# Attention with two value products in every second step, exponentials ahead of a copy, and a sixth buffer of probabilities

## The chip, the cores and the metric

The kernel runs on one core of a Trainium2 chip. The metric is device time in microseconds (us) for one launch. Before the change the median of 3 runs is 656.25 us (653.67 to 657.86).

## What is computed

An attention with a mask from hashed buckets, followed by two mixtures of experts on its output. Cut to what matters:

```python
# q, k, v: (2, 8, 768, 64) float32, proj: (64, 6)
q_bucket = sum((q @ proj > 0) * 2 ** arange(6))      # k_bucket likewise
scores = where(q_bucket == k_bucket, q @ k.T / 8, -1e9)
attn = exp(scores - max(scores)); attn = attn / (sum(attn) + 1e-9)
x = (attn @ v)            # laid out as 1536 rows of 512
x = moe(x)                # 8 experts, 192 rows each, assigned greedily by logit
out = moe2(x)             # rows with a positive skip score go to their best expert
```

## The kernel before, in words

Only the attention loop and three small places behind it are touched.

**Units and steps.** The 16 heads of queries are worked as 16 units (line 106): a pair of heads (two times 64 rows of the 128 partitions) and half of the 768 queries. A unit has 6 steps (line 354), each for 128 queries of one head against all 768 keys. One step issues, in program order:

- the scores, four matmuls in the first precision half (line 191) and the second (line 193), into a tile `S` of PSUM with 2 buffers; VectorE then takes the maximum (line 195) and two small numbers `g` and `b` (lines 196 and 197);
- splits of later queries and keys on VectorE and GpSimd (lines 130, 139, 146), by the tables `splits` and `kplan`;
- one chunk of the product with the values, `av` (line 227): a chunk is 128 keys, for both heads at once, two matmuls that fill 64 columns of the array each. After the sixth chunk ScalarE copies the result to `OT` (line 231) and VectorE computes `r` (lines 233 and 234);
- the projections for the buckets of the next unit (line 162, tile `aux`) in step 3, in some units also in step 1; VectorE turns them into bits (lines 168 and 176, "thresholds" below);
- transposes of the probabilities of two earlier steps (line 213), in tiles `pT` of PSUM with 2 buffers. One tile takes four transposes. An even step fills two tiles, an odd step one. ScalarE copies each to `PT` (line 216);
- the exponential of the step's own scores on ScalarE (line 204), which writes the probabilities `P`, 5 buffers.

In an even step the exponential stands between the copies of the two tiles. In an odd step it stands behind the copy of the one tile. Transposes of a pair of steps 2n and 2n+1 are issued in steps 2n+4 (two tiles) and 2n+5 (the third). In step 0 of units 3 to 15 a product `fin` (line 270) follows.

**What sets the order.** Each engine executes its instructions in the order in which this program issues them; the tile framework adds semaphores where a tile is written and read, or where a buffer is taken again.

**Behind the loop.** `consts` of class `Moe` (line 1070) fills part of a table `ys` in memory with zeros. `columns0` (line 1376) turns the first 128 rows of the second mixture's second tile. `tile2` (line 1397) computes one tile of the second mixture: `o` (line 1441) is the result, `ix` and `ixi` (lines 1444 and 1446) are the rows to which it goes, and `send` writes it out.

Of the kernel before, what the change touches and what calls it, by code (L numbers as in the profile page):

```python
# [7 lines left out]
F32 = mybir.dt.float32  # L8
# [5 lines left out]
ALU = mybir.AluOpType  # L14
# [9 lines left out]
class Net:  # L24
# [68 lines left out]
    def attention(self, r, later):  # L93

        nc, A = self.nc, self.A
        with self.rows as ctx:
# [2 lines left out]

            self.X = ctx.enter_context(self.pool("rows", 1)).tile([128, 12, XW], F32, name="X")  # L100
            st = ctx.enter_context(self.pool("st", 4))
            pp = ctx.enter_context(self.pool("pp", 5))
            ptp = ctx.enter_context(self.pool("ptp", 2))
            sm = ctx.enter_context(self.pool("sm", 4))
            ps = ctx.enter_context(self.pool("ps", 1, PSUM))
# [247 lines left out]
            for u in range(NU):  # L353
                for i in range(6):
                    g = u * 6 + i
                    score(u, i)
                    if (u, i) in setup:
                        setup[u, i]()
                    for f, *x in splits.get((u, i), []):
                        f(*x, ceng=nc.scalar if u == 0 else nc.vector)  # L360
                    if i == 1:
                        if u + 2 < NU:
                            loadq(u + 2)
                        for _ in kplan.get(u + 1, []):
                            if nload < len(order):
                                loadk(order[nload])
                                loadv(order[nload])
                                nload += 1
                    ua, ca = (u - 1, i - 4) if i >= 4 else (u - 2, i + 2)
                    if ua >= 0:  # L370
                        av(ua, ca)

                    if i and gens and (i == 1 or u == NU - 1 or not full[0]):
                        full[0] = next(gens[0], self)
                        if full[0] is self:
                            gens.pop(0)
                            full[0] = None
                    if left:
                        next(left, None)
                        left = None  # L380
                    if (u, i) in projs:
                        left = project(projs[u, i])
                        next(left, None)

                    gp = g - 4 if g % 2 == 0 else g - 5
                    if gp >= 0:
                        tu, ti = divmod(gp, 6)
                        for cp in ((0, 1) if g % 2 == 0 else (2,)):
                            tpose(tu, ti // 2, cp)
                            if cp == 0:  # L390
                                expo(u, i)
                    if gp < 0 or g % 2:
                        expo(u, i)
                    if i == 0 and u >= 3:
                        fin(u - 3)
                        if u - 3 in (6, 7, 11):
                            q = 3 * (6, 7, 11).index(u - 3)
                            gens.append(r.count0(q, q + 3, sm, ps, ("pT", 2, "aux")))
# [16 lines left out]
            g = r.count0(9, 11, sm, ps, tags)  # L415
# [3 lines left out]
            x = [fin_values(L - 2, UD[L]["A"][:, 384:768]), fin_values(L - 1, UD[L]["B"][:, 384:768])]  # L419
# [646 lines left out]
class Moe:  # L1066
# [3 lines left out]
    def consts(self):  # L1070
        n, nc, c = self.n, self.nc, self.n.c
        kw = dict(allow_small_or_imprecise_dtypes=True)

        self.wsg = c.tile([128, 4, 32], F32, name="wsg")
        nc.gpsimd.memset(self.wsg, 0.0)
        nc.sync.dma_start(self.wsg[:, :, 0:9], n.A["wsg"])
        self.i9 = c.tile([128, 9], F32, name="i9")
        v = nc.gpsimd
        v.tensor_tensor(self.i9, n.idf[:, 0:9], n.idf[:, 32:41], op=ALU.add)
        v.tensor_tensor(self.i9, self.i9, n.idf[:, 64:73], op=ALU.add)  # L1080
        v.tensor_tensor(self.i9, self.i9, n.idf[:, 96:105], op=ALU.add)
        self.cnt = c.tile([128, 8], F32, name="cnt2")
        nc.gpsimd.memset(self.cnt, 0.0)
        self.ecap = c.tile([128, 8], F32, name="ecap")
        nc.gpsimd.iota(self.ecap, pattern=[[1536, 8]], base=0, channel_multiplier=0, **kw)
        self.trash = c.tile([128, 1], F32, name="trash")
        nc.gpsimd.iota(self.trash, pattern=[[0, 1]], base=100000, channel_multiplier=1, **kw)
        self.par1 = c.tile([128, 1], F32, name="par1")
        nc.gpsimd.iota(self.par1, pattern=[[0, 1]], base=1, channel_multiplier=1, **kw)
        self.first = c.tile([128, 8, NB], F32, name="first")  # L1090
        nc.gpsimd.iota(self.first, pattern=[[0, 8], [128, NB]], base=128, channel_multiplier=0, **kw)
        nc.gpsimd.iota(self.first[:, 0:1, :], pattern=[[0, 1], [128, NB]], base=256, channel_multiplier=0, **kw)
        self.slot0 = c.tile([128, 2], F32, name="slot0")
        nc.gpsimd.iota(self.slot0, pattern=[[128, 2]], base=0, channel_multiplier=1, **kw)
        nc.gpsimd.iota(self.slot0[64:128, 1:2], pattern=[[0, 1]], base=128, channel_multiplier=1, **kw)

        with self.tc.tile_pool(name="zr", bufs=1, side="right") as zp:
            z = zp.tile([128, 386], F32, name="zrow")
            nc.gpsimd.memset(z, 0.0)
            zt = zp.tile([128, TROWS // 128, 4], F32, name="ztab")  # L1100
            nc.gpsimd.memset(zt, 0.0)
            nc.gpsimd.iota(zt.bitcast(I32)[:, :, 0], pattern=[[0, TROWS // 128]], base=1536, channel_multiplier=0)
            nc.sync.dma_start(n.A["tb"].rearrange("(p r) c -> p r c", p=128), zt)

            ys = n.A["ys"][1344:1537, :].rearrange("r d -> (r d)").rearrange("(h p x) -> h p x", h=2, p=128)
            for h in range(2):
                nc.sync.dma_start(ys[h], z)

    def fetch(self, res, half, q=None):

# [265 lines left out]
    def columns0(self, rows):  # L1376
# [6 lines left out]
        yield  # L1383
        for d in range(4):
            nc.tensor.matmul(pt[:, d, :], self.yr[0][:, d * 128:(d + 1) * 128], self.pick[:, 0, :], start=False, stop=False, **kw)
            nc.tensor.matmul(pt[:, d, :], self.yr[1][:, d * 128:(d + 1) * 128], self.pick[0:64, 1, :], start=False, stop=True, **kw)
        self.x0 = self.parts(pt)

# [8 lines left out]
    def tile2(self, W, rows, x, tick, nxt=None, last=False):  # L1397
# [36 lines left out]
        for f in range(8):  # L1434
# [2 lines left out]
                turn(1)  # L1437
            if f == 5 and nxt is not None:
                nx = nxt()
        o = self.m2.tile([128, 512], F32, name="o9") if last else sb.tile([128, 512], F32, name="o2", tag="yr1", bufs=2)  # L1440
        v.scalar_tensor_tensor(o, py, tb[:, 2:3], xr, op0=ALU.mult, op1=ALU.add)

        ix = sb.tile([128, 2], F32, name="ix")
        v.tensor_scalar(ix[:, 0:1], tb[:, 1:2], 0.5, self.trash, op0=ALU.is_lt, op1=ALU.mult)
        ixi = (self.m2 if last else sb).tile([128, 1], I32, name="ixi9" if last else "ixi")
        v.scalar_tensor_tensor(ixi, tb[:, 1:2], -1.0, ix[:, 0:1], op0=ALU.add, op1=ALU.add)
        if last:
            return o, ixi
        self.send(o, ixi)
# [275 lines left out]
```

## Time and profile before

| what | value |
|---|---|
| runs | 656.25 us median (653.67, 656.25, 657.86) |
| profiled execution | 658.05 us, of which span 656.3 us |
[...]
| PE (matmul) busy | 607.8 us, 93% of the span |
| PEld (weight load) busy | 423.6 us, 65% |
| DVE busy | 487.2 us, 74% |
| ACT busy | 399.7 us, 61% |
| POOL busy | 158.1 us, 24% |

The span is the time from the first to the last instruction; the 1.75 us around it are the same launch. PE is TensorE, PEld its weight loads, DVE is VectorE, ACT is ScalarE, POOL is GpSimd. A row of the timeline gives the start, the time taken, the engine, the line, the instruction with output and inputs, their shapes, how many instructions are merged in the row, and in brackets the idle time before it with what ended it. The scores of the first unit start at 7.5 us and the last step's at 257.45 us; the attention is done at about 280 us, and the two mixtures follow.

### The profile page before, as it was taken

Reading aid. Unit: us, or ns where it says so; the run is one execution under the profiler, and the core shown is the slowest. Engines: PE = TensorE matmul, PEld = TensorE weight load, DVE = VectorE, ACT = ScalarE, POOL = GpSimd, SP = SyncE. Lnnn points to the kernel's source line nnn. Section 1 sums busy time; section 2 is a strip of 40 time slices with the busy share of each in tenths; the row PEclk is TensorE's granted clock in tenths of the full one; section 3 lists DMA queues with packets and bytes.
Section 4 is the critical chain, followed back from the end, with each engine's and each line's share of the span. In section 5 each row is a group of like instructions: output and inputs, shape, how many; then the busy total and the mean of one; then the engine's idle time right before and its main releaser. Section 6 shows DMA issues by size and latency. Waiting matters only on the chain.

```text
span 656.3 us, 11406 instructions
## 1 busy us (share of the span) xinstructions
PE 607.8 (93%) x3781; PEld 423.6 (65%) x3781; DVE 487.2 (74%) x1542; ACT 399.7 (61%) x909; POOL 158.1 (24%) x212
## 2 busy tenths in 40 slices
PE   6999999999999999865878899999999999999994
PEld 3656665555566656745647486686786778877883
DVE  6888888889786786574848676867643567999991
ACT  5777777776777777412434554554554556887881
POOL 2343233332111110250103031221502322311110
PEclk8899999999999999957989899999999999999998
DMA  6214323312300010053367827558665379999800
GB/s 216 64 60 124 116 76 98 97 38 73 98 25 25 1 50 2 1 201 131 129 188 273 280 39 281 171 176 265 223 218 178 109 278 344 384 379 330 299 14 23
DMA packets 53239, 99.69 MB, mean 152 GB/s; under 512 B 6421, under 2 KB 12949, under 8 KB 53168
## 3 DMA queue, kind: packets, MB, share of 16 engines
q1 hardware_dynamic: 42016, 76.21, 35.0%
q10 hardware_dynamic: 7072, 13.63, 6.0%
q0 software_dynamic: 4080, 8.99, 4.2%
q8 instruction: 34, 0.56, 0.3%
q14 instruction: 37, 0.30, 0.2%
HBM read 88.72 MB, written 12.46 MB: 154 GB/s over the span
## 4 chain that ended last, share of the span: by engine, by line
PE 30%; DVE 10%; issue 6%; DMA 4%; ACT 2%; POOL 1%; POOLq 0%; ACTq 0%; DVEq 0%
PE ph L1166 10%; PE y L1191 6%; PE y L1197 4%; DVE wlo L1353 4%; DMA out<-o,ixi 3%; DMA xg<-xd,idsb 1%; PE pr L1235 1%; PE py L1414 1%; PE py L1413 1%; PE py L1412 1%; PE ph L1412 1%; PE pxt L1145 1%; PE ph L1413 1%; PE ph L1414 1%; ACT whi L1352 1%
## 5 line engine op out<-in xcount | busy, mean ns | idle before, releaser
L1353 DVE TENSOR_TENSOR wlo<-w,whi 128x512 fp32r<-128x512 f32 x192 | 123.6, 685 | 22.6 <-ACT whi L1352 20.8
L216 ACT ACTIVATE PT<-pT 128x512 f32<-128x512 f32 x135 | 79.8, 595 | 52.8 <-PE pT L213 52.1
L195 DVE TENSOR_REDUCE nm<-S 128x1 f32<-128x768 f32 x96 | 91.8, 956 | 25.9 <-PE S L193 24.1
L1352 ACT ACTIVATE whi<-w 128x512 fp32r<-128x512 f32 x192 | 109.4, 622 | 0.4 <-issue 0.4
L1166 PE MATMUL ph<-xT,w 128*128 128x192 f32 x512 | 103.0, 345 | 4.5 <-PEq L1518 4.5
L204 ACT ACTIVATE P<-S,b,g 128x768 f32<-128x768 f32 x96 | 94.7, 987 | 13.3 <-DVE b L197 11.7
L213 PEld LDWEIGHTS pT<-idf,P 128*128 128x128 f32 x576 | 62.4, 142 | 51.4 <-issue 30.7
L1166 PEld LDWEIGHTS ph<-xT,w 128*128 128x128 f32 x512 | 84.1, 195 | 14.9 <-issue 10.2
L213 PE MATMUL pT<-idf,P 128*128 128x128 f32 x576 | 84.7, 282 | 0.7 <-ACT PT L219 0.3
L227 PE MATMUL av<-PT,vd 128*64 128x384 f32 x360 | 77.5, 511 | 0.0
L191 PE MATMUL S<-K,Q 128*128 128x512 f32 x192 | 58.7, 387 | 5.3 <-ACT P L204 4.1
L146 POOL TENSOR_TENSOR Q<-qd,Q 64x384 fp32r<-64x384 f32 x30 | 31.0, 1033 | 134.2 <-PE pT L213 73.1
L1171 ACT ACTIVATE h<-ph 128x128 f32<-128x128 f32 x64 | 17.7, 276 | 60.0 <-PE ph L1166 30.7
L193 PE MATMUL S<-K,Q 76*128 76x512 f32 x192 | 51.0, 347 | 1.8 <-DVE Q L168 1.8
L191 PEld LDWEIGHTS S<-K,Q 128*128 128x128 f32 x192 | 29.7, 194 | 10.6 <-issue 5.8
L193 PEld LDWEIGHTS S<-K,Q 76*128 76x128 f32 x192 | 30.4, 195 | 6.4 <-issue 2.1
L139 POOL TENSOR_TENSOR K<-kd,K 64x768 fp32r<-64x768 f32 x15 | 27.2, 1815 | 26.3 <-DVE K L130 14.5
L1197 PE MATMUL y<-w,h 128*64 128x512 f32 x128 | 33.2, 624 | 0.0
L227 PEld LDWEIGHTS av<-PT,vd 128*64 128x64 f32 x360 | 18.0, 134 | 22.7 <-issue 19.2
L1314 POOL DMA_INDIRECT tb<-rec,ii x16 | 15.9, 996 | 64.7 <-DVE cnt L1311 48.5
L1414 PE MATMUL py<-whi,hl 128*128 128x512 f32 x72 | 29.3, 407 | 1.4 <-DVE hl L1423 1.3
L1412 PE MATMUL py<-whi,hh 128*128 128x512 f32 x72 | 29.9, 415 | 0.0
(374 smaller groups left out, 1100.6 us busy)
## 6 DMA issues: line engine op xcount, KB each, us to landing
w<-w SPq DMA_DIRECT2D x28, 1024.0 KB, 8.5
w<-u SPq DMA_DIRECT2D x26, 1024.0 KB, 9.6
kd<-kT SPq DMA_DIRECT2D x16, 384.0 KB, 4.7
qd<-qT SPq DMA_DIRECT2D x32, 192.0 KB, 3.8
w<-u ACTq DMA_DIRECT2D x6, 1024.0 KB, 13.2
w<-w ACTq DMA_DIRECT2D x4, 1024.0 KB, 7.6
xd<-X SPq DMA_DIRECT2D x4, 780.0 KB, 4.2
vd<-v SPq DMA_DIRECT2D x16, 192.0 KB, 4.0
```

Of the source, the lines that this page charges most:

```text
L191: nc.tensor.matmul(S[:, n0:n1], d["Q1", a][:, ts], kd["K1"][:, n0:n1], start=True, stop=False)
L193: nc.tensor.matmul(S[:, n0:n1], d["Q2", a][:, ts], kd["K2"][:, n0:n1], start=False, stop=True)
L195: nc.vector.tensor_reduce(d["nm"][:, c], S, op=ALU.max, axis=AX.X, negate=True)
L204: nc.scalar.activation(P, S, AF.Exp, bias=d["b"][:, c], scale=d["g"][:, c], accum_out=d["s"][:, c])
L213: nc.tensor.transpose(p[:, a, b, :], d["P"][2 * ip + b][:, (2 * cp + a) * 128:(2 * cp + a + 1) * 128], self.idf)
L216: nc.scalar.activation(dst, p.rearrange("p a b q -> p a (b q)"), AF.Copy)
L227: nc.tensor.matmul(d["av"][64 * a:64 * a + 64, :], VH[b * 8 + 2 * p + a][:, c, :], d["PT"][:, c, a * 384:(a + 1) * 384], start=(c == 0), s ...
L1166: nc.tensor.matmul(ph, w1[f // 4][:, d, f % 4 * 128:f % 4 * 128 + 128], xT[:, d, :], start=(d == 0), stop=(d == 3))
L1197: nc.tensor.matmul(y2[64 * h:64 * h + 64, :], h2[:, 4 * h + f, :], res["w2"][h][:, f, :], start=(f == 0), stop=(f == 3))
L1352: nc.scalar.activation(hi[:, c, :], w[:, c, :], AF.Copy)
L1353: nc.vector.tensor_tensor(lo[:, c, :], w[:, c, :], hi[:, c, :].bitcast(F32), op=ALU.subtract)
L1412: nc.tensor.matmul(out, a[0][:, i, :], hi[:, i % 4, :], start=start, stop=False)
```

## The change

In the attention loop: the value product is issued in odd steps alone, two chunks at a time. In odd steps the exponential is issued ahead of the transposes and of their copy. `P` has 6 buffers. Behind it: the zeros for `ys` come from a tile that is there anyway, by two other transfers, and one clearing on GpSimd is gone; `columns0` issues its four products with 128 rows first and then the four with 64; `tile2` computes `ix` and `ixi` ahead of `o`.

```diff
-            pp = ctx.enter_context(self.pool("pp", 5))
+            pp = ctx.enter_context(self.pool("pp", 6))
...
-                    ua, ca = (u - 1, i - 4) if i >= 4 else (u - 2, i + 2)
-                    if ua >= 0:
+
+                    ua, ca = (u - 1, 0) if i == 5 else (u - 2, i + 1)
+                    if i % 2 and ua >= 0:
                         av(ua, ca)
+                        av(ua, ca + 1)
...
                     gp = g - 4 if g % 2 == 0 else g - 5
+
+                    if gp < 0 or g % 2:
+                        expo(u, i)
                     if gp >= 0:
                         tu, ti = divmod(gp, 6)
                         for cp in ((0, 1) if g % 2 == 0 else (2,)):
                             tpose(tu, ti // 2, cp)
                             if cp == 0:
                                 expo(u, i)
-                    if gp < 0 or g % 2:
-                        expo(u, i)
...
-            z = zp.tile([128, 386], F32, name="zrow")
-            nc.gpsimd.memset(z, 0.0)
...
-            ys = n.A["ys"][1344:1537, :].rearrange("r d -> (r d)").rearrange("(h p x) -> h p x", h=2, p=128)
-            for h in range(2):
-                nc.sync.dma_start(ys[h], z)
+            ys = n.A["ys"][1344:1537, :].rearrange("r d -> (r d)").rearrange("(p x) -> p x", p=128)
+            z = n.zero.bitcast(F32)
+            nc.sync.dma_start(ys[:, 0:768].rearrange("p (k x) -> p k x", k=6), z[:, None, :].to_broadcast([128, 6, 128]))
+            nc.sync.dma_start(ys[:, 768:772], z[:, 0:4])
...
         for d in range(4):
             nc.tensor.matmul(pt[:, d, :], self.yr[0][:, d * 128:(d + 1) * 128], self.pick[:, 0, :], start=False, stop=False, **kw)
+        for d in range(4):
             nc.tensor.matmul(pt[:, d, :], self.yr[1][:, d * 128:(d + 1) * 128], self.pick[0:64, 1, :], start=False, stop=True, **kw)
...
-        o = self.m2.tile([128, 512], F32, name="o9") if last else sb.tile([128, 512], F32, name="o2", tag="yr1", bufs=2)
-        v.scalar_tensor_tensor(o, py, tb[:, 2:3], xr, op0=ALU.mult, op1=ALU.add)
 
         ix = sb.tile([128, 2], F32, name="ix")
         v.tensor_scalar(ix[:, 0:1], tb[:, 1:2], 0.5, self.trash, op0=ALU.is_lt, op1=ALU.mult)
         ixi = (self.m2 if last else sb).tile([128, 1], I32, name="ixi9" if last else "ixi")
         v.scalar_tensor_tensor(ixi, tb[:, 1:2], -1.0, ix[:, 0:1], op0=ALU.add, op1=ALU.add)
+        o = self.m2.tile([128, 512], F32, name="o9") if last else sb.tile([128, 512], F32, name="o2", tag="yr1", bufs=2)
+        v.scalar_tensor_tensor(o, py, tb[:, 2:3], xr, op0=ALU.mult, op1=ALU.add)
```

ScalarE from step 4 of unit 6 to step 0 of unit 7, before (`pT` is a tile of transposes, its number tells which; `P` is the exponential's output):

```order
L216 ACTIVATE PT_1419<-pT_1420 128x2x256
L204 ACTIVATE P_1426,s_1265<-S_1406,b_1264,g_1263 128x768
L216 ACTIVATE PT_1419<-pT_1428 128x2x256
L216 ACTIVATE PT_1419<-pT_1444 128x2x256
L204 ACTIVATE P_1450,s_1265<-S_1434,b_1264,g_1263 128x768
L216 ACTIVATE PT_1419<-pT_1471 128x2x256
L204 ACTIVATE P_1477,s_1455<-S_1456,b_1454,g_1453 128x768
L216 ACTIVATE PT_1419<-pT_1479 128x2x256
```

and with the change:

```order
L216 ACTIVATE PT_1414<-pT_1415 128x2x256
L204 ACTIVATE P_1421,s_1263<-S_1404,b_1262,g_1261 128x768
L216 ACTIVATE PT_1414<-pT_1423 128x2x256
L204 ACTIVATE P_1442,s_1263<-S_1429,b_1262,g_1261 128x768
L216 ACTIVATE PT_1414<-pT_1444 128x2x256
L216 ACTIVATE PT_1414<-pT_1467 128x2x256
L204 ACTIVATE P_1473,s_1453<-S_1454,b_1452,g_1451 128x768
L216 ACTIVATE PT_1414<-pT_1475 128x2x256
```

The exponential of step 5 (the second `L204`) now stands ahead of the copy of step 5's one tile (`pT_1444` in both).

TensorE from step 4 of unit 6 to step 0 of unit 7, before (`x2` and `x4` count matmuls in a row; a chunk of `av` is two):

```order
L193 MATMUL S<-K_1163,Q_1128 128x512
L193 MATMUL S<-K_1163,Q_1128 128x256
L227 MATMUL av<-PT,vd 64x384 x2
L213 MATMUL pT<-idf,P 128x128 x8
L191 MATMUL S<-K_1162,Q_1127 128x512
L191 MATMUL S<-K_1162,Q_1127 128x256
L193 MATMUL S<-K_1163,Q_1128 128x512
L193 MATMUL S<-K_1163,Q_1128 128x256
L227 MATMUL av<-PT,vd 64x384 x2
L213 MATMUL pT<-idf,P 128x128 x4
```

and with the change:

```order
L193 MATMUL S<-K_1161,Q_1124 128x512
L193 MATMUL S<-K_1161,Q_1124 128x256
L213 MATMUL pT<-idf,P 128x128 x8
L191 MATMUL S<-K_1160,Q_1123 128x512
L191 MATMUL S<-K_1160,Q_1123 128x256
L193 MATMUL S<-K_1161,Q_1124 128x512
L193 MATMUL S<-K_1161,Q_1124 128x256
L227 MATMUL av<-PT,vd 64x384 x4
L213 MATMUL pT<-idf,P 128x128 x4
```

The even step loses its value product; the odd step has two chunks in one piece.

## Rows read from the trace of the kernel before

**Rows 1.** Busy us by engine in two stretches; columns PE, PEld, DVE, ACT, POOL, clock, DMA, GB/s

```profile
48.00:250.00 202.00, 200.38 (x1283) 120.88 (x1281) 168.82 (x430) 145.83 (x283) 54.42 (x85) 1.00 0.21 67
...
560.00:580.00 20.00, 19.98 (x95) 15.58 (x94) 19.80 (x39) 17.99 (x34) 4.23 (x4) 1.00 1.05 389
```

**Rows 2.** Timeline of PE, unit 8, steps 2 to 4; start, us, instruction

```profile
137.48 0.87 PE L227 MATMUL av<-PT,vd 128*64 128x384 f32 x4
138.27 1.09 PE L213 MATMUL pT<-idf,P 128*128 128x128 f32 x8
139.12 0.59 PE L191 MATMUL S<-K,Q 128*128 128x512 f32 x2
...
139.99 0.87 PE L227 MATMUL av<-PT,vd 128*64 128x384 f32 x4
...
141.55 0.66 PE L213 MATMUL pT<-idf,P 128*128 128x128 f32 x4
141.96 0.60 PE L191 MATMUL S<-K,Q 128*128 128x512 f32 x2
```

**Rows 3.** Timeline of PE, unit 0, step 5: transposes right behind scores

```profile
22.03 0.60 PE L191 MATMUL S<-K,Q 128*128 128x512 f32 x2
...
22.82 0.60 PE L213 MATMUL pT<-idf,P 128*128 128x128 f32 x4
```

**Rows 4.** Timeline of PE behind the loop: three chunks of values in one piece

```profile
263.09 2.16 PE L227 MATMUL av<-PT,vd 128*64 128x384 f32 x12
265.08 1.48 PE L312 MATMUL S<-PT,vd 128*64 128x128 f32 x24
```

**Rows 5.** Timeline of PE and DVE, unit 6, steps 3 to 5

```profile
106.95 0.59 PE L191 MATMUL S<-K,Q 128*128 128x512 f32 x2
...
107.93 0.96 DVE L195 TENSOR_REDUCE nm<-S 128x1 f32<-128x768 f32 x1 [0.39 <-PE S L193]
...
109.11 0.34 DVE L197 TENSOR_TENSOR b<-g,nm 128x1 f32<-128x1 f32 x1
...
112.90 1.25 DVE L176 TENSOR_SCALAR K<-aux,thr 12x384 fp32r<-12x384 f32 x2
...
115.36 0.16 DVE L197 TENSOR_TENSOR b<-g,nm 128x1 f32<-128x1 f32 x1
```

**Rows 6.** Timeline of ACT, unit 6, steps 2 and 5

```profile
107.29 0.99 ACT L204 ACTIVATE P<-S,b,g 128x768 f32<-128x768 f32 x1
...
108.25 0.59 ACT L216 ACTIVATE PT<-pT 128x512 f32<-128x512 f32 x1
...
113.95 1.33 ACT L216 ACTIVATE PT<-pT 128x512 f32<-128x512 f32 x2
115.62 0.99 ACT L204 ACTIVATE P<-S,b,g 128x768 f32<-128x768 f32 x1 [0.34 <-DVE b L197]
```

**Rows 7.** Timeline of PE and ACT, unit 1, step 0; then PE's waits, 23 to 48 us

```profile
24.40 1.04 PE L213 MATMUL pT<-idf,P 128*128 128x128 f32 x8
26.23 0.62 PE L191 MATMUL S<-K,Q 128*128 128x512 f32 x2 [0.80 <-ACT P L204]
...
25.10 0.99 ACT L204 ACTIVATE P<-S,b,g 128x768 f32<-128x768 f32 x1 [0.66 <-DVE b L197]
...
PE S L191 <- ACT P L204: 1.9, 4, 0.8
```

**Rows 8.** Timeline of PE in `columns0`

```profile
534.35 1.05 PE L1382 MATMUL pxt<-idf,xr 128*128 128x128 f32 x8
535.24 0.39 PE L1385 MATMUL pxt<-pick,yr 128*128 128x128 f32 x2
...
538.48 0.66 PE L1421 MATMUL pht<-idf,hr 128*128 128x128 f32 x4
```

**Rows 9.** Timeline of DVE at the last tile's end

```profile
647.56 0.75 DVE L1441 SCALAR_TENSOR_TENSOR o<-py,tb,xr 128x512 f32<-128x512 f32 x1 [2.87 <-PE py L1414]
...
648.46 0.16 DVE L1446 SCALAR_TENSOR_TENSOR ixi<-tb,ix 128x1 int32<-128x1 f32 x1
```

## The prediction

> **What bounds the kernel now.** I read the stretches first. From 48 to 250 us, the undisturbed part of the attention, TensorE is busy 200.38 of 202 us at full clock, VectorE 168.82, ScalarE 145.83, GpSimd 54.42, the DMA engines a fifth [rows 1]. So the order of work on TensorE sets the attention's time, with VectorE (84%) close behind it. Then I read the timeline of TensorE for what each block costs, always from its start to the start of the next block, since the rows' own durations overlap. One step is: scores 0.87 (139.12 to 139.99), one chunk of values 0.79 (137.48 to 138.27), transposes 0.85 for two tiles (138.27 to 139.12) or 0.41 for one (141.55 to 141.96), projections 0.76 where there are any (from 139.99 + 0.80 to 141.55) [rows 2]. Last I read VectorE and ScalarE over the same steps for how late an exponential comes, since the change puts a copy behind it.
>
> Is a busy share of 99% the end of it? [...] By the busy share regrouping the same matmuls would give 0; by the start-to-start rows it gives what the next paragraph works out, and I take the rows.
>
> **The value products: -11.6 us.** Three chunks in one piece took 1.99 us (263.09 to 265.08), 0.66 each, against 0.79 alone [rows 4, 2]. Transposes right behind scores started 0.79 us after them (22.03 to 22.82) instead of 0.87 for values, and four took 0.60 instead of 0.66 [rows 3, 2]. So an even step without values is 0.79 + 0.79 = 1.58 instead of 0.87 + 0.79 + 0.85 = 2.51, a gain of 0.93, and the odd step gets 0.66 more: 0.27 gained for each pair of steps. There are 43 such pairs (1 in unit 1, 3 in each of units 2 to 15): 11.6 us. The ends: with 0.79 for the second chunk as well, 0.14 a pair or 6.0 us; with nothing paid between blocks (0.60 a chunk, from 1.99 less 0.79 over two), 0.33 or 14.2 us.
>
> **The copy behind the exponential: +15.4 us.** ScalarE executes in order. In an even step the second tile's copy (108.25) already waits behind the exponential that started at 107.29, though its transposes stand ahead of the scores of 106.95 on TensorE [rows 5, 6]. So an odd step's copy now starts 0.96 us (one exponential) after that exponential's start. [...]
>
> Who waits for that copy? `pT` has two buffers, so the second tile of the next even step takes the buffer that this copy empties, and TensorE stands there, with everything behind it.
>
> *Step 5 of a unit with a new head's keys.* In unit 6 the scores of step 3 start at 106.95. VectorE then works without a gap from the maximum at 107.93 over the splits and the four thresholds (the last two 1.25 us at 112.90) to the `b` of step 5 at 115.36, and the exponential starts at 115.62, 8.67 after those scores [rows 5, 6]. This chain doesn't change and doesn't wait for TensorE after the change either. TensorE, counted from the same scores: step 3 is 0.87 + 0.79 + 0.66 + 0.76 + 0.41 = 3.49, step 4 1.58, step 5 0.87 + 1.45 + 0.41 = 2.73, so step 0 begins at 7.80, its first tile at 8.59, its second at 9.03 if free (four transposes behind it at 0.11 each, from 0.89 for eight such matmuls [rows 8]). The copy starts at 8.67 + 0.96 = 9.63 and ends 0.59 later [rows 6], at 10.2. TensorE waits 1.2 us, where before the copy started ahead of the exponential (second of the two at 113.95) and nobody waited. Keys come in units 0 to 9; for units 2 to 9 that is 8 x 1.2 = 9.6 us. The ends: 0 if VectorE's chain were short enough, 8 x 1.6 if it gets 0.4 longer.
>
> *The other odd steps.* Without that backlog `b` comes 1.18 after the maximum (107.93 to 109.11), the maximum 0.98 after the scores, the exponential 0.26 after `b`: 2.42, the copy from 3.38 to 3.98. The next second tile wants the buffer at 2.73 + 0.79 + 0.44 = 3.96. The two meet; I count 0.05 for some 20 places, 1.0 us. Where a projection lies in the odd step there are 0.76 us to spare, which also cover the `OT` copy that step 3 now has ahead of its exponential. In units 10 and 14 pieces of the router's counting stand in VectorE's order at these steps; I take 1.2 us for each, 2.4, between 0 and 3.2.
>
> *Units 0 and 1*, with hardly any values to fill the odd step. The exponential of unit 0's step 5 starts at 25.10, the copy would end at 25.10 + 0.96 + 0.60 = 26.66, and the second tile of the next step, due at 24.40 + 0.44 = 24.84, waits till then. Scores follow 0.36 later, at 27.0, instead of 26.23 where before they waited for the exponential: +0.8 [rows 7]. Two more such pairs in unit 1 give the same each: 2.4 us, less at most the 1.9 us that TensorE waits there before, so between 0.5 and 3.
>
> The loop in sum: -11.6 + 9.6 + 1.0 + 2.4 + 2.4 = **+3.8 us**. The sixth buffer gives time to nobody by itself: an odd step's exponential would without it wait for the transposes that now stand behind it.
>
> **The small places: -0.7 us.** In `columns0` the eight products take 3.24 us (535.24 to 538.48), alternating between 128 and 64 rows; eight matmuls of one kind right ahead took 0.89. Two groups of 0.89 and two changes of kind at 0.1 to 0.2 make 2.0, a gain of 1.2 on TensorE [rows 8]. But behind it VectorE is busy 19.80 of 20 us and the DMA engines are full [rows 1], so I count 0.4, between 0 and 1.2. At the end the send waited for `ixi` (done at 648.62) and will wait for `o` (done at 648.31): 0.3 us [rows 9]. In the other tiles VectorE does the same work in another order: 0. The clearing on GpSimd and the smaller transfers to `ys` lie in a stretch where GpSimd is busy 27% and the DMA engines 21% [rows 1]: 0; if that cover were gone, some tenths.
>
> The sum is +3.1 us: 658.05 becomes 661.2 in the profiled execution's own time. That execution is 1.8 above the median of the runs, so on the median I forecast **659 us**.
>
> **The rivals.** *A, faster:* the copy behind the exponential is ready in time and the gain on TensorE stays. For it speaks that in the odd steps without keys the two meet within 0.02 us, and ScalarE has room (72%). Against it the gapless chain of unit 6, which units 3 to 8 repeat. It gives -11.6 + 2.4 - 0.7, that is 646 us. Chance 0.15. *B, clearly slower:* the copy misses not one tile in a unit but nearly all. The margin of the ordinary odd step is 3.96 against 3.98; if VectorE is 0.3 us later there, by `b` at 0.34 instead of 0.16 [rows 5] or a split ahead of the maximum, each of some 25 places costs 0.3 more, 7.5 us: 666 us. It decides from about 0.15 us on. Chance 0.10. *C, the regrouping is worth nothing on TensorE* (the second chunk in a piece costs as much as one alone and the transposes gain little): the gain is 6.0 instead of 11.6, so 665 us. Against it the 1.99 us of [rows 4]. Chance 0.05.
>
> **How the numbers follow.** The likeliest case has 0.70; its own range is 656 to 663. About 1% (6.6 us) is what a measurement of this kernel can tell from no change: 649.7 to 662.8. Faster by more has A's 0.15, slower by more the 0.15 of B and C, the same 0.70 of the forecast. The range for 8 in 10 is 648 to 665: it leaves out the far end of A and of B.
>
> **What would show it.** In the profile after: values in rows of 8 matmuls with 1.4 to 1.5 us from start to start; waits of TensorE's transposes (line 213) for the copy of line 216, about 1.2 us each, at the start of units 2 to 10, and next to none in units 11 to 13; units 3 to 8 longer by 0.2 to 0.5 us each, from the scores of step 0 to the next, and units 11 to 13 shorter by 0.7; the loop's last scores some 4 us later. Wrong would be: no such waits (then A), or waits at steps 2 and 4 as long as at step 0 (then B).

## The result, and the profile after

| | before | with the change |
|---|---|---|
| median of 4 runs each | 657.06 us (653.67 to 658.35) | 665.45 us (663.61 to 667.24) |
| ratio | 1 | 1.0136 [1.0087, 1.0184] |
| profiled execution (span) | 658.05 (656.3) us | 667.24 (665.3) us |
| mean granted TensorE clock (1 is full) | 0.964 | 0.958 |
| scores of the first step to scores of the last | 249.95 us | 257.78 us |

The kernel is slower by 1.4%. The forecast of 659 had the sign (+2.75 on the median of 656.25) and about a third of the size, and 665.45 lies just above the range. The two profiled executions differ by 9.2 us; 7.8 of them lie in the attention loop, where the forecast had 3.8.

The stretch of [rows 1] again, after the change (columns: busy us of PE, PEld, DVE, ACT, POOL, then clock, DMA share, GB/s):

```profile
48.00:250.00 202.00, 188.50 (x1255) 122.30 (x1253) 166.38 (x417) 143.26 (x275) 56.27 (x93) 1.00 0.22 67
```

TensorE now stands still for 13.5 of these 202 us at full clock (202 less 188.50), against 1.6 before. What it waits for says the view of the waits, 12 to 275 us, of the kernel after (us in total, times, longest):

```profile
ACT P L204 <- DVE b L197: 51.2, 59, 1.7
...
PE pT L213 <- ACT PT L216: 19.8, 14, 2.0
```

The second row is new: before the change no transpose waited for the copy of line 216 in this stretch. The forecast put 15.4 us on this copy; 14 waits took 19.8. The first row says what ScalarE waits for now: VectorE's `b`, 51.2 us against 11.7 before, when it waited for the transposes ahead of their copy instead (52.1 us, now 11.1). Now the same stretch of work as in [rows 2, 5, 6], unit 6 from step 3 on, in the kernel after. First PE:

```profile
112.24 0.59 PE L191 MATMUL S<-K,Q 128*128 128x512 f32 x2
...
113.11 1.51 PE L227 MATMUL av<-PT,vd 128*64 128x384 f32 x8
114.55 0.50 PE L162 MATMUL aux<-qd,prs 64*12 64x384 f32 x2
...
115.73 0.60 PE L191 MATMUL S<-K,Q 128*128 128x512 f32 x2
116.16 0.52 PE L193 MATMUL S<-K,Q 76*128 76x512 f32 x2
116.52 1.21 PE L213 MATMUL pT<-idf,P 128*128 128x128 f32 x8
117.49 0.59 PE L191 MATMUL S<-K,Q 128*128 128x512 f32 x2
...
120.22 0.60 PE L191 MATMUL S<-K,Q 128*128 128x512 f32 x2
...
121.02 0.60 PE L213 MATMUL pT<-idf,P 128*128 128x128 f32 x4
123.19 0.66 PE L213 MATMUL pT<-idf,P 128*128 128x128 f32 x4 [1.57 <-ACT PT L216]
```

Two chunks of values take 1.44 us from start to start (113.11 to 114.55), and transposes start 0.79 behind scores (115.73 to 116.52), both as forecast. The eight transposes of this even step take 0.97 us to the next scores (116.52 to 117.49), where the forecast had 0.79. Then, in step 0 of unit 7, the second tile, due 0.44 after the first at 121.46, starts at 123.19: TensorE stands for 1.7 us. The forecast had 1.2 here. Then ACT, same kernel and view:

```profile
121.57 0.99 ACT L204 ACTIVATE P<-S,b,g 128x768 f32<-128x768 f32 x1 [1.11 <-DVE b L197]
...
122.55 1.07 ACT L216 ACTIVATE PT<-pT 128x512 f32<-128x512 f32 x2
```

The exponential of step 5 starts at 121.57, 9.33 us after step 3's scores (112.24) instead of 8.67; the copy that TensorE waits for stands right behind it at 122.55, as forecast. Why 0.66 later? DVE, then POOL:

```profile
112.90 0.55 DVE L130 CAST K<-kd 128x768 fp32r<-128x768 f32 x1
113.37 0.95 DVE L195 TENSOR_REDUCE nm<-S 128x1 f32<-128x768 f32 x1
114.35 0.15 DVE L196 TENSOR_SCALAR g<-nm 128x1 f32<-128x1 f32 x1
114.54 0.82 DVE L197 TENSOR_TENSOR b<-g,nm 128x1 f32<-128x1 f32 x1
115.29 0.55 DVE L130 CAST K<-kd 128x768 fp32r<-128x768 f32 x1
...
121.29 0.16 DVE L197 TENSOR_TENSOR b<-g,nm 128x1 f32<-128x1 f32 x1
```

```profile
113.53 1.81 POOL L139 TENSOR_TENSOR K<-kd,K 64x768 fp32r<-64x768 f32 x1 [2.54 <-DVE K L130]
```

Step 3's `b` takes 0.82 us and ends at 115.36; GpSimd's subtraction of the new keys' second half ends at 115.34 (113.53 + 1.81). The same place in the kernel before, DVE, then POOL:

```profile
106.98 0.55 DVE L130 CAST K<-kd 128x768 fp32r<-128x768 f32 x1
```

```profile
107.61 1.81 POOL L139 TENSOR_TENSOR K<-kd,K 64x768 fp32r<-64x768 f32 x1 [2.20 <-DVE K L130]
```

There the subtraction ended at 109.42 and the `b` of 0.34 us [rows 5] at 109.45, so it was held too, but only for 0.18 us; in units 2 to 5 `b` took 0.16. What changed is when the scores come. Before, they started 0.03 us ahead of the copy of the keys (106.95 and 106.98), and the maximum had 0.39 us of idle time ahead of it, ended by those scores. Now they start 0.66 ahead of it (112.24 and 112.90); the maximum follows the copy without a gap, 1.13 us after the scores instead of 0.98, and `b`, two instructions on, runs into the subtraction earlier. The subtraction starts 0.08 us after VectorE's copy ends (113.45 and 113.53; before 107.53 and 107.61), so it doesn't come earlier with the scores.

The small places. PE in `columns0`, kernel after, as in [rows 8]:

```profile
545.62 1.06 PE L1387 MATMUL pxt<-pick,yr 128*128 128x128 f32 x8
546.61 1.16 PE L1389 MATMUL pxt<-pick,yr 64*128 64x128 f32 x8
547.69 0.66 PE L1424 MATMUL pht<-idf,hr 128*128 128x128 f32 x4
```

The eight products take 2.07 us (545.62 to 547.69) instead of 3.24. From the start of these products to the start of the last `o` it is 111.27 us instead of 112.32, so 1.05 of the 1.2 is kept. From that start to the end of the span it is 8.41 instead of 8.72, the 0.3 of the forecast.

### The profile page after: what moved, and what is told of

Read it like the earlier page. It is cut to its first block, busy times and chain, and to the rows that moved or that the text cites. A ratio compares the mean times of both kernels' runs of the same rounds, so it can differ in the third digit from the quotient of the medians.

```text
span 665.3 us, 11410 instructions
## 1 busy us (share of the span) xinstructions
PE 603.8 (91%) x3781; PEld 432.9 (65%) x3781; DVE 489.3 (74%) x1542; ACT 402.0 (60%) x909; POOL 158.3 (24%) x211
## 4 chain that ended last, share of the span: by engine, by line
PE 27%; DVE 9%; issue 8%; DMA 5%; ACT 2%; POOL 1%; POOLq 0%; ACTq 0%
PE ph L1168 9%; PE y L1193 5%; DVE wlo L1355 4%; PE y L1199 4%; DMA out<-o,ixi 3%; DMA xg<-xd,idsb 2%; PE py L1417 1%; PE pr L1237 1%; PE ph L1415 1%; PE py L1416 1%; PE py L1415 1%; PE ph L1416 1%; PE ph L1417 1%; ACT whi L1354 1%; PE pxt L1147 1%
## 5 line engine op out<-in xcount | busy, mean ns | idle before, releaser
L204 ACT ACTIVATE P<-S,b,g 128x768 f32<-128x768 f32 x96 | 95.3, 992 | 57.8 <-DVE b L197 51.2
L1168 PE MATMUL ph<-xT,w 128*128 128x192 f32 x512 | 106.0, 352 | 4.2 <-PEq L1521 4.2
L213 PE MATMUL pT<-idf,P 128*128 128x128 f32 x576 | 88.1, 282 | 20.3 <-ACT PT L216 19.8
L213 PEld LDWEIGHTS pT<-idf,P 128*128 128x128 f32 x576 | 64.3, 142 | 55.1 <-ACT PT L216 27.1
L1168 PEld LDWEIGHTS ph<-xT,w 128*128 128x128 f32 x512 | 86.5, 200 | 14.7 <-issue 9.9
L216 ACT ACTIVATE PT<-pT 128x512 f32<-128x512 f32 x135 | 78.5, 593 | 11.8 <-PE pT L213 11.1
L227 PE MATMUL av<-PT,vd 128*64 128x384 f32 x360 | 68.0, 499 | 0.0
L227 PEld LDWEIGHTS av<-PT,vd 128*64 128x64 f32 x360 | 21.8, 136 | 27.3 <-issue 27.0
L1316 POOL DMA_INDIRECT tb<-rec,ii x16 | 16.6, 1040 | 64.2 <-DVE cnt L1313 48.0
```

Source lines behind the costliest of these rows:

```text
L204: nc.scalar.activation(P, S, AF.Exp, bias=d["b"][:, c], scale=d["g"][:, c], accum_out=d["s"][:, c])
L213: nc.tensor.transpose(p[:, a, b, :], d["P"][2 * ip + b][:, (2 * cp + a) * 128:(2 * cp + a + 1) * 128], self.idf)
L216: nc.scalar.activation(dst, p.rearrange("p a b q -> p a (b q)"), AF.Copy)
L227: nc.tensor.matmul(d["av"][64 * a:64 * a + 64, :], VH[b * 8 + 2 * p + a][:, c, :], d["PT"][:, c, a * 384:(a + 1) * 384], start=(c == 0), s ...
L1168: nc.tensor.matmul(ph, w1[f // 4][:, d, f % 4 * 128:f % 4 * 128 + 128], xT[:, d, :], start=(d == 0), stop=(d == 3))
```

## The experiments

Each ran beside runs of the kernel before on its own chip (medians 656.04, 657.51, 656.95 and 657.58 us); ratios are against those.

### The two parts apart

*Values in pairs alone*: the change with the exponential of odd steps behind the copy again (six buffers and the small places stay).

```diff
-                    if gp < 0 or g % 2:
+                    ahead = False
+                    if gp < 0 or g % 2 and ahead:
                         expo(u, i)
...
+                    if gp >= 0 and g % 2 and not ahead:
+                        expo(u, i)
```

> The changed kernel with the copy ahead of the exponential in odd steps again, as before; the values stay two chunks in every second step. Theory (the copy behind the exponential is what costs): no wait of the transposes for line 216 at the units' starts. But the copy now waits for transposes that stand behind two chunks, the exponential behind the copy ends about 4.5 us after the odd step's start, and the scores two steps later want its buffer at 4.3: 0.2 to 0.3 us of waiting in some 30 odd steps, 8 us of the 11.6 gained. About 653 us, 4 below before. Rival 1 (grouping the values itself costs time, by a tile or a buffer held longer): 660 or more, with the waits of line 213 still there. Rival 2 (nothing else waits, the whole gain stays): 644.

Measured: 653.83 us (652.89 to 655.33), ratio 0.9957 [0.9938, 0.9975]. Its waits of TensorE:

```profile
PE S L191 <- ACT P L204: 5.7, 19, 1.2
```

No transpose waits for line 216. But of the 0.81 us that three pairs free in a unit, units 3 to 8 are only 0.12 to 0.14 shorter (15.19 to 15.21 and 15.95 to 15.97 us instead of 15.33 and 16.09). ACT in unit 6 shows why:

```profile
105.54 0.60 ACT L216 ACTIVATE PT<-pT 128x512 f32<-128x512 f32 x1 [2.10 <-PE pT L213]
106.03 0.99 ACT L204 ACTIVATE P<-S,b,g 128x768 f32<-128x768 f32 x1
```

The pair of chunks delays the odd step's transposes, so the exponential behind their copy comes later, and the scores two steps on wait for its buffer. In unit 6 the scores of steps 3 and 5 start 1.20 and 1.12 us behind the transposes ahead of them (106.06 to 107.26, 111.54 to 112.66) instead of 0.79, 0.74 of the 0.81; the view of the waits shows only part of this. Regrouping without the exponential ahead loses most of its gain in the loop: 247.8 us instead of 249.95.

*The exponential ahead alone*: the kernel before with six buffers and the exponential ahead in odd steps.

```diff
+                    if gp < 0 or g % 2:
+                        expo(u, i)
                     if gp >= 0:
...
-                    if gp < 0 or g % 2:
-                        expo(u, i)
```

> The kernel before with two edits alone: six buffers of probabilities, and the exponential ahead of the transposes and their copy in odd steps. Theory: the wait for the copy needs no regrouped values. In a unit with a new head's keys the second tile of step 0 comes 2.10 us after the step's start instead of 1.23, so the wait is 1.7 - 0.6 = 0.7 to 1.1 us in 8 units, and units 0 and 1 lose 1.5: +7 to +9, 664 us. Rival (only the values in odd steps make the copy late): no such waits, 657.

Measured: 665.94 us (664.7 to 668.39), ratio 1.0138 [1.0095, 1.0181]: all of the loss, and about what was expected. Its waits, then the DVE row that answers to the one at 113.37 above, and POOL:

```profile
PE pT L213 <- ACT PT L216: 8.7, 11, 1.7
```

```profile
112.08 0.96 DVE L195 TENSOR_REDUCE nm<-S 128x1 f32<-128x768 f32 x1 [0.38 <-PE S L193]
```

```profile
111.77 1.81 POOL L139 TENSOR_TENSOR K<-kd,K 64x768 fp32r<-64x768 f32 x1 [2.20 <-DVE K L130]
```

With the values still in every step, the maximum again waits 0.38 us for TensorE and comes 0.31 behind the subtraction's start, `b` takes 0.33 to 0.35 in units 6 to 8, and the exponential of step 5 starts 8.69 to 8.72 after step 3's scores, as before. The pairs alone do lengthen it. DVE in unit 6 of that run:

```profile
109.43 0.55 DVE L197 TENSOR_TENSOR b<-g,nm 128x1 f32<-128x1 f32 x1
```

`b` takes 0.55 to 0.57 there in units 2 to 8, and the exponential of step 5 starts 8.91 to 8.93 after step 3's scores in units 6 to 8. So the regrouping begins the hold, and the hold of 0.8 comes from both parts together: the shortened even step brings the scores early, and the early scores find GpSimd in the way. No run has the sixth buffer alone. In the profiled loops the parts are -2.2 us (247.79) and +8.5 (258.41), both together +7.8: the sum of the parts, +6.3, lacks 1.5.

### The copy behind the exponential only where it is ready

The change, but the exponential stands ahead only in steps 1 and 3, and from unit 2 on.

```diff
-                    if gp < 0 or g % 2:
+                    ahead = u >= 2 and i != 5
+                    if gp < 0 or g % 2 and ahead:
                         expo(u, i)
...
+                    if gp >= 0 and g % 2 and not ahead:
+                        expo(u, i)
```

> The changed kernel, with the exponential ahead of the copy only in steps 1 and 3 from unit 2 on; in step 5 and in units 0 and 1 the copy goes first as before. Theory (the loss is the copy of step 5 behind an exponential that VectorE makes late): the 19.8 us of waits for line 216 fall to under 3; the scores of step 1 may wait some tenths for the exponential of step 5. About 648 us, 9 below before. Rival (ScalarE and VectorE are simply full, and the wait moves elsewhere, to scores that wait for exponentials): 658 to 665.

Measured: **647.80 us** (647.53 to 648.39), ratio 0.9870 [0.9829, 0.9911]. Its waits:

```profile
PE S L191 <- ACT P L204: 3.3, 7, 0.7
...
PE pT L213 <- ACT PT L216: 1.0, 1, 1.0
```

One wait of 1.0 us is left of fourteen. The exponential of step 5 comes just as late as in the change (9.30 to 9.31 in units 6 to 8), but the copy stands ahead of it and nobody needs it yet. The loop takes 241.2 us, 16.6 less than with the change; 12.5 of these lie in units 3 to 10 and 2.1 in units 0 to 2, where units 0 and 1 have the old order in every step. This kernel is faster than the kernel before and the change, and than the pairs alone (653.83) too: ahead in steps 1 and 3 the exponential does what the pairs need, in step 5 of the units with new keys it costs.

### A shorter chain to step 5

The change with the second two thresholds of a new key issued behind step 5's maximum instead of ahead of it.

```diff
-                    if left:
+                    if left and i != 4:
```

> The changed kernel with the second half of a projection's thresholds (two, 1.25 us on VectorE) issued one step later: behind the maximum of step 5, no longer ahead of it. Nothing else moves. Theory (VectorE's chain of steps 3 to 5 sets when step 5's exponential starts, and with it the copy): the exponential of step 5 starts 1.2 us earlier, the wait at the start of units 2 to 10 falls from about 1.7 to 0.5 us, 9 to 10 us less than the changed kernel: 655 to 656. Rival (the copy is late for ScalarE's own sake, or TensorE waits for something else): the waits stay at 1.7, 665.

Measured: 651.0 us (649.28 to 654.4), ratio 0.9933 [0.9903, 0.9964], better than the 655 to 656 expected. Its waits:

```profile
PE pT L213 <- ACT PT L216: 8.1, 11, 1.7
```

The exponential of step 5 starts 8.11 after step 3's scores in units 6 to 8, 1.22 earlier than in the change, and these units are 15.95 us long instead of 17.16 to 17.18: 1.21 to 1.23 shorter. Step 3's `b` still takes 0.82. So what the chain loses here, TensorE gets back one for one.

*Both edits together:*

> The changed kernel with both remedies: the exponential ahead of the copy only in steps 1 and 3 from unit 2 on, and the second half of a projection's thresholds one step later. Theory: the first remedy has taken away the waits at the units' starts already (1.0 us is left in that run), so the second finds little: the scores' waits for step 5's exponential, 1 us at most: 646 to 648. Rival (the two add up, 17.6 and 14.4 us): 633.

Measured: 648.41 us (645.32 to 649.38), ratio 0.9853 [0.9825, 0.9881]. The gains don't add: each removes the same wait.

### Is VectorE held by GpSimd?

*Shorter subtractions*: the change with the key subtraction in four pieces of 192 columns.

```diff
-                    eng.tensor_tensor(K2[0:64, c], d["k"][0:64, c], K1[0:64, c].bitcast(F32), op=ALU.subtract)
+                    for m in range(4 if n == 1 and ceng is nc.vector else 1):
+                        ...
+                        eng.tensor_tensor(K2[0:64, e], d["k"][0:64, e], K1[0:64, e].bitcast(F32), op=ALU.subtract)
```

> The changed kernel with GpSimd's subtraction for a head's keys (1.81 us, line 139) in four pieces of 192 columns. Nothing else moves. In the changed kernel VectorE's b of step 3 took 0.82 us instead of 0.16 while that subtraction ran (b 114.54 to 115.36, the subtraction 113.53 to 115.34), and the wait at the start of unit 8 was 1.57 to 1.73 us where I had reckoned 1.2. Theory (b is held until GpSimd's instruction ends): with pieces b is held for one piece at most, 0.1 to 0.4 us; the wait falls by 0.3 to 0.5 in the eight units 2 to 9, 3 to 4 us less than the changed kernel, 662 us. Rival (b is late for another reason, or GpSimd gets in again between VectorE's instructions): b at step 3 stays at 0.8, the time at 665.

Measured: 665.0 us (664.41 to 665.75), ratio 1.0114 [1.0086, 1.0142]: a miss by 3 us. DVE, then POOL, unit 6 (lines stand 3 further down in this kernel):

```profile
116.78 0.16 DVE L200 TENSOR_TENSOR b<-g,nm 128x1 f32<-128x1 f32 x1
116.86 0.55 DVE L130 CAST K<-kd 128x768 fp32r<-128x768 f32 x1
117.33 0.56 DVE L236 TENSOR_SCALAR r<-s 128x6 f32<-128x6 f32 x1
```

```profile
115.78 4.85 POOL L142 TENSOR_TENSOR K<-kd,K 64x192 fp32r<-64x192 f32 x8 [2.66 <-DVE K L130]
...
116.88 0.98 POOL L142 TENSOR_TENSOR K<-kd,K 64x192 fp32r<-64x192 f32 x1
```

The last row is the third piece, seen by itself. `b` is free at 0.16, but now `r`, two instructions later, takes 0.56 instead of 0.16 and ends 0.03 us after that piece (117.89 and 117.86). Seven pieces take 0.58 to 0.60 us and the third 0.98, having started with VectorE's copy (116.86 to 117.41); together 4.85 for the two keys instead of 2 x 1.81. The chain gets shorter by 0.27 in units 6 to 8 (9.06), not by 0.6, and units 7 and 8 are 0.27 to 0.28 shorter. The piece size moved the hold more than it removed it.

Unit 6 is 18.67 us long, 1.5 more than in the change, most of it at a lower granted clock. Stretches of this run (columns as above):

```profile
104.00:107.00 3.00, 1.31 (x11) 1.03 (x10) 2.61 (x8) 1.93 (x4) 0.38 (x1) 1.00 0.01 2
107.00:110.50 3.50, 3.50 (x16) 2.92 (x16) 0.90 (x3) 1.59 (x4) 1.09 (x3) 0.51 0.00 0
```

TensorE stood for 1.69 us at the start of unit 6 with the granted clock at 1.00, and in the 3.5 us after that the clock was 0.51: `fin` and the scores behind it take 1.28 and 1.58 us to the next start, against 0.64 and 0.89 in unit 7. The change has waits as long (up to 2.0 us) and a clock of 1.00 over 48 to 250 us. So 1.3 of these 1.5 us of the profiled execution lie in blocks at the lower clock (0.64 + 0.69); the miss stays without them.

*Another form of b*: one tensor input and `g` as the scalar operand.

```diff
-                nc.vector.tensor_tensor(d["b"][:, c], d["g"][:, c], d["nm"][:, c], op=ALU.mult)
+                nc.vector.tensor_scalar(d["b"][:, c], d["nm"][:, c], d["g"][:, c], None, op0=ALU.mult)
```

> The change with one instruction written in another form: b = g * nm is a tensor_scalar (one tensor input, g as the scalar operand) instead of a tensor_tensor with two inputs. Theory, part one: b of step 3 takes 0.8 us because VectorE's two-input form is held while GpSimd's subtraction runs; so here it takes 0.15 to 0.2 in units 3 to 8. Theory, part two: this hold is what lengthened the chain to step 5's exponential, so it comes 0.5 to 0.6 us earlier (8.7 to 8.8 after step 3's scores in units 6 to 8 instead of 9.33), TensorE's waits for the copy fall from about 1.7 to 1.1 each, and 7 units x 0.55 = 4 us are saved: 661. Rival one: the hold is not on the form, and the split's copy behind b, the next in VectorE's order, is held instead: chain 9.3, 665. Rival two: b isn't held by GpSimd at all, but waits for g: b stays 0.8, 665.

Measured: 665.38 us (664.91 to 665.88), ratio 1.0135 [1.0111, 1.0159]. Rival one holds. DVE, then POOL:

```profile
115.25 0.21 DVE L197 TENSOR_SCALAR b<-nm,g 128x1 f32<-128x1 f32 x1
115.38 1.08 DVE L130 CAST K<-kd 128x768 fp32r<-128x768 f32 x1
```

```profile
114.24 1.81 POOL L139 TENSOR_TENSOR K<-kd,K 64x768 fp32r<-64x768 f32 x1 [2.54 <-DVE K L130]
```

`b` passes while the subtraction runs, at 0.21. The copy behind it then takes 1.08 instead of 0.55 and ends at 116.46, 0.41 after GpSimd's end at 116.05. The exponential of step 5 comes at 9.41 to 9.42. So the hold isn't tied to `b`: where `b` passes, the copy behind it is held. The version of 647.8 us with this form of `b`:

> The version with the exponential ahead only in steps 1 and 3, with the same other form of b. Nobody waits there for step 5's copy, so an earlier b should give next to nothing: 647 to 648. Rival: TensorE still waits for VectorE at the scores (for the exponential or the maximum), and 0.5 us in each of 7 units come back: 644.

Measured: 649.16 us (646.77 to 650.29), ratio 0.9882 [0.9858, 0.9907], against 0.9870 [0.9829, 0.9911] without it: no gain within the runs' spread, as expected, though the median lies above the 647 to 648 named.

*No subtraction*: for heads 8 to 15 GpSimd's key subtraction is left out, and VectorE's work stays as it is.

```diff
-                K2 = d["K2"] = kp.tile([76, 768], F32R, name="K2")
+                K2 = d["K2"] = kp.tile([76, 768], F32R, name=f"K2h{g}", bufs=1) if g < 8 else KH[g - 8]["K2"]
...
-                    eng.tensor_tensor(K2[0:64, c], d["k"][0:64, c], K1[0:64, c].bitcast(F32), op=ALU.subtract)
+                    if g < 8:
+                        eng.tensor_tensor(K2[0:64, c], d["k"][0:64, c], K1[0:64, c].bitcast(F32), op=ALU.subtract)
```

> The change without GpSimd's key subtraction for heads 8 to 15, whose second precision half takes the rows of the head eight before (so the output is off for that half): units 6 to 9 have no 1.81 us subtraction in steps 2 and 3, units 2 to 4 keep theirs as a control in the same run. VectorE's copies and thresholds all stay. Theory (VectorE is held until GpSimd's subtraction ends): in units 6 to 8 step 3's b takes 0.16 and the copy behind it 0.55, the exponential of step 5 comes about 0.66 earlier (8.7 after step 3's scores instead of 9.33), each unit from 6 to 8 is about 0.6 shorter (16.6 instead of 17.17), and units 2 to 4 stay (8.7, 8.7, 9.5). In sum 4 x 0.65 = 2.6 us: 662.8. Rival (VectorE's own work is what makes the chain, and the hold only fills time in which it would wait anyway): 9.3 and 17.2 in units 6 to 8 too, 665.4.

Measured: 662.1 us (658.67 to 664.38), ratio 1.007 [1.0042, 1.0099]. DVE in unit 6, then PE at the start of unit 7 (lines one further down):

```profile
112.56 0.55 DVE L130 CAST K<-kd 128x768 fp32r<-128x768 f32 x1
...
114.21 0.16 DVE L198 TENSOR_TENSOR b<-g,nm 128x1 f32<-128x1 f32 x1
114.28 0.55 DVE L130 CAST K<-kd 128x768 fp32r<-128x768 f32 x1
...
120.29 0.16 DVE L198 TENSOR_TENSOR b<-g,nm 128x1 f32<-128x1 f32 x1
```

```profile
120.51 0.60 PE L214 MATMUL pT<-idf,P 128*128 128x128 f32 x4
122.19 0.66 PE L214 MATMUL pT<-idf,P 128*128 128x128 f32 x4 [1.08 <-ACT PT L217]
```

The exponential of step 5 starts 8.67, 8.66 and 8.66 after step 3's scores in units 6 to 8; in units 2 to 4, which keep the subtraction, it is 8.71, 8.69 and 9.50 (8.73, 8.70 and 9.49 in the change). The second tile, due at 120.95, starts at 122.19, so TensorE stands 1.24 us. Units 7 and 8 are 16.51 us long, 0.66 less than with the change and 0.42 more than before. This run has the chain of 8.67, the wait of 1.2 and the lengthening "by 0.2 to 0.5" that the prediction named for the change itself. That it is 8.67 again is in part luck: the maximum still starts 1.13 after the scores, 0.15 later than before, and `b` is 0.18 shorter than before.

*The same piece left out of the kernel before:*

> The kernel before with the same piece left out (no key subtraction for heads 8 to 15). Theory: b of step 3 took 0.33 there in units 6 to 8, so its chain gains at most 0.18 (8.5 instead of 8.67), no transpose waits for a copy, and the time stays within 1 us: 656 to 657. Rival (the subtraction costs time whatever the order of the exponential, through TensorE's waits for new keys): 653 to 655.

Measured: 655.75 us (653.54 to 659.22), ratio 0.9975 [0.9953, 0.9998]. That is 1.6 us less by the ratio, where "within 1 us" was expected. The chain is 8.50 instead of 8.67, and units 7 and 8 stay at 16.09. So the subtraction costs those units nothing where no copy stands behind the exponential; unit 9, where a key and the router's counting meet, is 1.07 shorter, and the whole loop 1.0 (248.96).

### The small places alone

The kernel before with the edits behind the loop, as the change's diff has them.

> The kernel before with the edits outside the attention loop alone: columns0 in two groups, ix and ixi ahead of o, the zeros of ys from another tile. Theory (by the two profiles: columns0 2.07 instead of 3.24 us on TensorE, 1.05 of it left at the end; the send 0.31 earlier): 1.4 us less than before. Rival (the DMA engines and VectorE bound that stretch and give the 1.05 away): 0.3 less.

Measured: 655.48 us (652.12 to 658.23), ratio 0.9963 [0.9943, 0.9983], that is 2.4 us less by the ratio (0.37% of 657.51) and 2.0 by the medians. PE in `columns0`:

```profile
533.58 1.06 PE L1384 MATMUL pxt<-pick,yr 128*128 128x128 f32 x8
534.57 1.16 PE L1386 MATMUL pxt<-pick,yr 64*128 64x128 f32 x8
535.65 0.66 PE L1421 MATMUL pht<-idf,hr 128*128 128x128 f32 x4
```

2.07 us again; from their start to the last `o` 111.30 us, and 8.41 from that to the end. The profile has 1.3 of the gain; the interval of the ratio runs from 1.1 to 3.7 us, so the rest isn't settled.

## Why the prediction was right in kind and wrong in size

The loop by stretches, each from scores to scores of step 0; the forecast's terms are put where their waits fall:

| units | forecast | measured |
|---|---|---|
| 0 to 2 | 2.4 - 4 x 0.27 = +1.3 | +1.8 |
| 3 to 10 (waits for step 5 of units 2 to 9) | 9.6 - 24 x 0.27 = +3.1 | **+8.4** |
| 11 to 13 | 1.2 - 9 x 0.27 = -1.2 | -1.9 |
| 14 to the last scores | 1.2 - 6 x 0.27 = -0.4 | -0.5 |
| other odd steps | +1.0 | in the rows above |
| sum | +3.8 | +7.8 |

**The value products: right.** A pair of chunks takes 1.44 us, transposes start 0.78 to 0.80 after scores, and where nobody waits the gain is there: units 11 to 13 are 0.57, 0.72 and 0.56 shorter, forecast 0.7. Rival C falls; that its 665 us is near the time is luck.

**The copy behind the exponential: right place, wrong size.** The waits stand at step 0 of units 2 to 10, between 1.0 and 2.0 us each, and none at units 11 to 13. Rival A falls.

**The step that failed** is in that term: "This chain doesn't change and doesn't wait for TensorE after the change either." I read the chain from step 3's scores as VectorE's own work and let it start earlier with the scores. In the rows it had a wait for TensorE in it, the 0.39 us ahead of the maximum, and a hold by GpSimd, the `b` at 0.34, which the text gives to rival B alone without asking what lengthened it. When the scores came early, that idle time didn't become a gain: VectorE ran into GpSimd's subtraction. From the copy of the keys to step 5's `b` it is 8.38 us before (106.98 to 115.36) and 8.39 after (112.90 to 121.29), and 7.73 without the subtraction (112.56 to 120.29). So the chain stayed tied to the copy and the subtraction while TensorE moved ahead of it, and from step 3's scores it measured 9.33 us instead of 8.67. Of the 0.66, 0.48 is the longer hold of `b` and 0.15 the maximum behind the copy.

Over units 2 to 9 the exponential of step 5 comes 4.8 us later in sum, counted from step 3's scores (0.47 to 0.67 a unit). With 4.8 the forecast's +3.1 for units 3 to 10 becomes +7.9; measured is +8.4. The term itself, put at 9.6, measured 12.2 in the eight waits at step 0 of units 3 to 10; the rest doesn't show as waiting, in part because TensorE came to the second tile later too (in unit 7 9.22 us after step 3's scores, forecast 9.03).

The run without the subtraction shows the cause: there the wait is 1.24 and the unit 0.42 longer. That is shown for units 6 to 8; for units 2 to 5 it rests on the same `b` of 0.78 to 0.8 there, which ends 0.02 us after the subtraction in each of units 2 to 8. In unit 9 (0.55) `b` is 0.16 and the maximum comes late instead; without the subtraction the chain there is 9.19 instead of 10.83. My upper end, "8 x 1.6 if it gets 0.4 longer", bounded the wrong amount: nothing in its working said how late GpSimd could make it.

**Rival B** gave 666, close to the time, and named `b`. But its mechanism isn't what the profile shows: it wanted 0.3 us at some 25 ordinary odd steps. From unit 2 on a single wait lies elsewhere than at step 0 (0.98 in unit 9), so that its 666 was near is luck. The margin of 0.02 us, counted as 1.0 us, held roughly: one even step in each of units 2 to 8, 11, 13 and 15 takes 0.95 to 0.97 us for its transposes instead of 0.79, too short a loss to stand among the waits, 1.6 us in ten places. What makes it I didn't separate.

**Units 0, 1 and the router.** Three waits of 1.72, 1.54 and 0.63 us in unit 1 stand where the text put them, and a fourth, 1.04 at the start of unit 2, where the sum had three in all. Units 0 to 2 cost 0.5 more than forecast. The router's piece in unit 14 made a wait of 1.67 at the start of unit 15; that of unit 10 made none.

**The small places.** Sent 0.3 earlier: right. `columns0` gave 1.05, not 0.4: I took VectorE's busy 19.80 of 20 us for a cover, but the rest of the mixture moved up with the products. The 0.1 to 0.2 for a change of kind was an estimate that no row of the kernel before shows; the two groups took 0.99 (545.62 to 546.61) and 1.08 us (546.61 to 547.69), against the 0.89 of the eight matmuls of one kind.

**Outside the loop** the profiled execution has 0.5 us more from the last scores to the first expert's first product (44.63 to 45.10), which I didn't follow, and 1.7 more in the first three experts. Their stretch before, then after:

```profile
302.08:398.93 96.85, 83.33 (x517) 61.16 (x517) 69.27 (x336) 44.81 (x133) 16.83 (x20) 0.95 0.58 189
310.66:409.22 98.56, 87.29 (x517) 64.39 (x517) 69.44 (x336) 44.96 (x133) 16.85 (x20) 0.90 0.58 186
```

The granted clock is 0.95 before and 0.90 after. No edit touches these experts, and over the profiles of the experiments they took from 94.0 us (at 0.96, the thresholds late) to 98.6 (at 0.90, the exponential ahead alone). So this goes with the clock that the execution was granted; what sets it there wasn't tried.

## What to carry to other kernels

A chain that looks gapless on one engine is only fixed if every instruction in it has its usual length and no idle time ahead of it: compare each with the same line elsewhere, and ask what the engine meets when its input comes early. Putting a copy behind an exponential paid here only in steps where the exponential is ready; with it in the late step of a unit as well, and in units 0 and 1, a gain of 1.3% became a loss of 1.4%. A gain on the busiest engine is worth what the next engine in the loop lets through (here 2.2 us in the loop of a forecast 11.6, with the values in pairs alone), so try the two parts of such a change apart and step by step.

## What the runs showed of the hardware

While GpSimd's subtraction ran (1.81 us for 64x768), some of VectorE's instructions were held and others passed. Held were `b` with two tensor inputs (0.16 to 0.82 us, ending 0.02 after the subtraction), the copy of 128x768 (0.55 to 1.08, ending 0.41 after it) and, with the subtraction in pieces, `r` (0.16 to 0.56, ending 0.03 after a piece). The maximum, which reads PSUM (0.95), `g` (0.15) and `b` in the form with a scalar operand (0.21) were not held. Where the subtraction was left out, `b` with two tensor inputs took 0.16 and the copy 0.55 at the same place (unit 6, step 3). What decides which of VectorE's instructions are held, no run here shows.

Cutting the GpSimd instruction in four made it longer, 1.81 to about 2.4 us for each key (4.85 over two), so shorter holds were paid with more of them. The piece that met VectorE's copy took 0.98 us instead of 0.58 to 0.60.

Eight products alternating between 128 and 64 rows took 3.24 us, in two groups of four 2.07 us, in both kernels that group them.
